# Six early weight tiles rounded by an integer addition instead of a float sum, in an attention kernel with two MLPs

## The chip, the cores and the metric

The kernel runs on one core of a Trainium2 chip. The metric is the device time of one execution in microseconds (us). Five engines work side by side, each through its own instructions in a fixed order: TensorE (PE; its weight loads are shown apart as PEld), VectorE (DVE), ScalarE (ACT), GpSimd (POOL) and SyncE (SP), which here starts most of the DMA transfers. An engine that waits for another holds back everything behind the waiting instruction in its own order.

## The reference

Attention goes through 32 memory slots per head: the key and value sums are weighted by a softmax over positions (`a`), the queries are scored against those slots, and the result `x` (4608 rows of 512) goes through a gated MLP and an ELU MLP. All inputs are float64 or float32; the three weight arrays arrive as float64.

```python
a = exp(phi - max(phi));  a = a / (sum(a) + 1e-9)
k_m = einsum('bhsm,bhsd->bhmd', a, k);  v_m = einsum('bhsm,bhsd->bhmd', a, v)
attn = softmax(q @ k_m.T / sqrt(64))
x = (attn @ v_m)                       # (8*576, 512)
x = (silu(x @ w_gate) * (x @ w_val)) @ w_out
h = x @ w_in;  return where(h > 0, h, exp(min(h, 0)) - 1) @ w_out2
```

## The kernel before

The eight batches go through a front part (`phi`, `a_T`, `kv_mm`, `kv_out`, `kv_T`: the softmax over positions and the small products that give `kT` and `vt`), a back part (`score`, `norm`, `attn`: the attention weights `at`), and the first MLP. The gate and value weights are first multiplied by `vt` (`vw`), so that the MLP's products take `at` directly (`gate1`, `val1`, through `up1`); `down1` multiplies the result by the output weights. Every large product is three products of split numbers (high by high, high by low, low by high). `vw(0, p)` of the first two pairs splits its result in PSUM: ACT copies the high part, PE subtracts it with a product by minus one (`minus`), ACT copies the rest.

A float64 weight is two 32-bit words. `words` (L122) makes a float32 pair from them: ACT reads the high word with a stride and scales it (L126); DVE shifts the exponent into place (L127), puts the sign back (L128), keeps the exponent alone (L130) and multiplies the low word by it (L131). The caller adds the two (`load_w`, L144), or, for the output weights of the first pass, splits them (`load_wo`, L171 to L173). The tiles of concern are the six that are decoded before PE is full: `wg` of pair 0 in four halves of 512 columns, `wg` of pair 1 in two tiles of 1024, and the two output tiles `wo` (in DVE's rows `wv`).

The program is written in Python order and a scheduler sets each engine's order. `tc.issue_after(x)` keeps what is written in its block behind `x`; `later()` is such a fence behind the last `h` and the first `ex`. In the first batch (`b == 0`) the list `todo` deals out the output tiles and the front part of batch 1 between the MLP's units (`tick`). Behind the second unit stands `spin` (L297): 13 products of `minus` by itself that nothing reads, then `vw(0, 1)`.

Of the kernel before, what the change touches and what calls it, by code (L numbers as in the profile page):

```python
# [8 lines left out]
F32 = mybir.dt.float32  # L9
F32R = mybir.dt.float32r  # L10
I32 = mybir.dt.int32
U32 = mybir.dt.uint32
# [26 lines left out]
def attention_moe_moe(ctx: ExitStack, tc: tile.TileContext, qT, phiT, kv, kv4, w1g, w1o, w2, out):  # L39
# [81 lines left out]
    def words(v, r):  # L121
# [9 lines left out]
        stt(out=cf, in0=lo32.bitcast(U32), scalar=2.0 ** -52, in1=cf, op0=ALU.mult, op1=ALU.mult)  # L131
        return cf

    def later():
        st = ExitStack()
        for after in last.get("h"), first.get("ex"):
            if after:
                st.enter_context(tc.issue_after(after.ins))
        return st

    def load_w(v, r):
        with later():
            cf = words(v, r)
            last["sum"] = tt(out=v, in0=v, in1=cf, op=ALU.add)  # L144

# [3 lines left out]
    def load_wg(p, k2, pool, parts=1):  # L149
        t = pool.tile([128, 2, 512], F32, tag="w", name="wg")  # L150
        WG[p][2 * k2], WG[p][2 * k2 + 1] = t[:, 0], t[:, 1]
        r = raw.pop((p, k2), None)
        if r is None:
            r = fetch_w(w1g[p, k2])
        t = t.rearrange("p i c -> p (i c)")
        n = 1024 // parts
        for i in range(parts):
            cs = slice(n * i, n * i + n)
            load_w(t[:, cs], r[:, cs])
        ahead((p, k2))  # L160

    def load_wo(u2, pool):
        hi = pool.tile([128, 2, 512], F32R, tag="w", name="woh")
        lo = (bk_p if u2 else pool).tile([128, 2, 512], F32R, tag="w", name="wol")
        for i in range(2):
            WO[2 * u2 + i] = hi[:, i], lo[:, i]
        hi, lo = (x.rearrange("p i c -> p (i c)") for x in (hi, lo))
        v = work("wv")
        with later():
            cf = words(v, fetch_w(w1o[u2]))  # L170
            act(out=hi, in_=v, func=AF.Copy)  # L171
            tt(out=v, in0=v, in1=hi.bitcast(F32), op=ALU.subtract)
            tt(out=lo, in0=v, in1=cf, op=ALU.add)  # L173

    SET = {}
    stores = []
# [53 lines left out]
    def vw(b, p, pool=None, ps=None):  # L230
        t = VW[b, p] = vx_p.tile([128, 2, 2, 512], F32R, tag="vx", name="vw")
        both = ps or pool.tile([128, 2, 512], F32, tag="at", name="pvw")
        ps = [both[:, g] for g in range(2)]

        def head(j, g):
            r, c = slice(64 * g, 64 * g + 64), slice(32 * j, 32 * j + 32)
            return mm(ps[g][c], lhsT=Bs[b].vt[r, j, :], rhs=WG[p][j][r], start=True, stop=True)

        together([lambda j=j, g=g: head(j, g) for j in reversed(range(KD)) for g in (1, 0)])
        if b >= NEG or p >= UA // 2:  # L240
            with tc.high_priority() if pool is None else nullcontext():
                act(out=t[:, 0], in_=both, func=AF.Copy)
                tt(out=t[:, 1], in0=both, in1=t[:, 0].bitcast(F32), op=ALU.subtract)
            return
        for g in range(2):
            act(out=t[:, 0, g, :], in_=ps[g], func=AF.Copy)
            mm(ps[g], lhsT=minus, rhs=t[:, 0, g, :], start=False, stop=True, skip_group_check=True)
            act(out=t[:, 1, g, :], in_=ps[g], func=AF.Copy)

    def up1(ps, w, c0, at, s0):  # L250
        cs, ss = slice(c0, c0 + 128), slice(s0, s0 + HS)
# [19 lines left out]
    def gate1(b, u, at, s0, silu):  # L271
        pg = ps_gv.tile([128, HS], F32, tag="g", name="pg")
        up1(pg, VW[b, u // 2], 256 * (u % 2), at, s0)
        s = t_p.tile([128, HS], F32, tag="s", name="s")
        if silu:
            last["gate"] = act(out=s, in_=pg, func=AF.Silu)
        else:

            act(out=s, in_=pg, func=AF.Tanh, scale=0.5)
            stt(out=s, in0=s, scalar=1.0, in1=pg, op0=ALU.add, op1=ALU.mult)  # L280
        return s

# [19 lines left out]
    class Batch:  # L302
# [18 lines left out]
        def phi(self):  # L321
            ph = self.ph
            nmx = fr_p.tile([128, 2], F32, tag="nmx", name="nmx")
            nc.vector.tensor_reduce(out=nmx, in_=ph, op=ALU.max, axis=AX.X, negate=True)
            sm = fr_p.tile([128, 2], F32, tag="sm", name="sm")
            for g in range(2):
                act(out=ph[:, g, :], in_=ph[:, g, :], func=AF.Exp, bias=nmx[:, g:g + 1],
                    accum_out=sm[:, g:g + 1])
            self.rs = fr_p.tile([128, 2], F32, tag="rs", name="rs", bufs=2)
            nc.vector.tensor_scalar_add(out=self.rs, in0=sm, scalar1=1e-9)  # L330
            nc.vector.reciprocal(out=self.rs, in_=self.rs)
# [3 lines left out]
        def a_T(self, c0):  # L335
            if c0 == 0:
                self.a = fr_p.tile([128, 9, 128], F32, tag="a", name="a")
            ps = ps_fr.tile([128, 4, 128], F32, tag="at", name="ps_aT")
            ph = self.ph.rearrange("p g s -> p (g s)")
            if c0 == 4:  # L340
                nc.tensor.transpose(out=ps[:, 0], in_=ph[:, 512:640], identity=ident)
                act(out=self.a[:, 8], in_=ps[:, 0], func=AF.Copy)
                return
            for i in range(2):
                for g in range(2):
                    s0 = 128 * (c0 + i) + 640 * g
                    nc.tensor.transpose(out=ps[:, 2 * i + g], in_=ph[:, s0:s0 + 128], identity=ident)
            act(out=self.a[:, 2 * c0:2 * c0 + 4], in_=ps, func=AF.Copy)


        def kv_mm(self, cs, start, stop):
# [22 lines left out]
        def kv_T(self):  # L374
            ps = ps_fr.tile([128, 2, 4, M], F32, tag="at", name="ps_kvT")
            for i in range(2):
                nc.tensor.transpose(out=ps[:, i].rearrange("p j m -> p (j m)"),
                                    in_=self.kvm[:, i].rearrange("p g d -> p (g d)"), identity=ident)
            self.kT = bk_p.tile([128, 4, M], F32, tag="kT", name="kT", bufs=2)
            act(out=self.kT, in_=ps[:, 0], func=AF.Copy)  # L380
            if self.b == 0:
                self.kTd = bk_p.tile([128, 4, 2, M], F32, tag="kTd", name="kTd")
                nc.gpsimd.memset(self.kTd, 0.0)
                for g in range(2):
                    r = slice(64 * g, 64 * g + 64)
                    act(out=self.kTd[r, :, g], in_=ps[r, 0], func=AF.Copy)
            self.vt = vt_p.tile([128, 4, M], F32, tag="vt", name="vt")
            act(out=self.vt, in_=ps[:, 1], func=AF.Copy)

# [43 lines left out]
        def attn(self, hf):  # L435
            if hf == 0:
                self.at = av_p.tile([128, 2, 2, S], F32R, tag="at", name="at")
            if self.b == 0 and hf == 1:
                t = ps_at.tile([128, 2, T], F32, tag="at", name="ps_ex")
                sc = self.sc.rearrange("p g s -> p (g s)")  # L440
                for i in range(2):
                    for g in range(2):
                        c0 = 256 * i + 128 * g
                        nc.tensor.transpose(out=t[:, g, 128 * i:128 * i + 128], in_=sc[:, c0:c0 + 128], identity=ident)
                for g in range(2):
                    c0 = 512 + M * g
                    last["ex"] = nc.vector.transpose(out=t[:, g, 256:HS], in_=sc[:, c0:c0 + M])
                t = t[:, :, :HS]
            else:
                t = bk_p.tile([128, 2, HS], F32, tag="ex", name="ex")  # L450
                last["ex"] = nc.vector.transpose(out=t.rearrange("p g s -> p (g s)"), in_=self.sc.rearrange("p g s -> p (g s)"))
            hi, lo = (self.at[:, i, :, HS * hf:HS * hf + HS] for i in range(2))
            act(out=hi, in_=t, func=AF.Copy)  # L453
            tt(out=lo, in0=t, in1=hi.bitcast(F32), op=ALU.subtract)  # L454

        def store_at(self):
# [99 lines left out]
    for b in range(B):  # L556
# [1 line left out]
        bk = list(back_tasks(b + 1)) if b + 1 < B else []  # L558
        fr = list(front_tasks(b + 2)) if b + 2 < B else []
        if b == 0:  # L560
            wo = [lambda u=u: load_wo(u, wo_p) for u in range(UA // 2)]
            pair = last["sum"]

            def phi1():
                with tc.issue_after(pair.ins):
                    Bs[1].phi()
                load_q(Bs[1])

            f1 = [phi1] + list(front_tasks(1)) + [lambda: Bs[2].phi()]
            for i in range(max(len(wo), len(f1))):  # L570
                todo += wo[i:i + 1] + f1[i:i + 1]
        if 2 <= b <= 5:
            bk += [lambda: load_wg(2 + (b - 2) // 2, b % 2, wa_p)]
        if b == B - 2:
# [29 lines left out]
        for hf in range(2):  # L604
            for u in range(UA):
# [2 lines left out]
                hs[hf, u] = val1(b, u, Bs[b].at, HS * hf, s, silu)  # L608
                tick()
                if (b, hf, u) == (0, 0, 1):  # L610
                    with tc.issue_after(last["pe"].ins):
                        spin(ps_kv, "at", 13)
                    vw(0, 1, G2)
                if prev:
                    down1(*prev.pop(0))
# [495 lines left out]
```

## Time and profile before

| what | value |
|---|---|
| median of 3 runs | 1432.77 us (1432.74 to 1434.7) |
| profiled execution | 1434.9 us, of which the span of the instructions is 1433.1 us |
| PE busy | 1407.0 us, 98% of the span |
| DVE busy | 1141.3 us, 80% |
| ACT busy | 857.7 us, 60% |
| mean granted clock of PE | 0.993 |
| chain that ended last | PE 89%, DMA 5%, DVE 4%, issue 1%, ACT 1% |

The profile comes from one execution. Times inside it are counted from the start of the span. PE's granted clock has two levels here, 1.0 (2.4 GHz) and 0.5 (1.2 GHz). A row of the timeline is the start, the duration, the engine, the line and operation, what is written from what with its shapes, and, where the engine stood idle before, for how long and who released it.

### The profile page before, as it was taken

Reading aid. Unit: us, or ns where it says so; the run is one execution under the profiler, and the core shown is the slowest. Engines: PE = TensorE matmul, PEld = TensorE weight load, DVE = VectorE, ACT = ScalarE, POOL = GpSimd, SP = SyncE. Lnnn points to the kernel's source line nnn. Section 1 sums busy time; section 2 is a strip of 40 time slices with the busy share of each in tenths; the row PEclk is TensorE's granted clock in tenths of the full one; section 3 lists DMA queues with packets and bytes.
Section 4 is the critical chain, followed back from the end, with each engine's and each line's share of the span. In section 5 each row is a group of like instructions: output and inputs, shape, how many; then the busy total and the mean of one; then the engine's idle time right before and its main releaser. Section 6 shows DMA issues by size and latency. Waiting matters only on the chain.

```text
span 1433.1 us, 23220 instructions
## 1 busy us (share of the span) xinstructions
PE 1407.0 (98%) x9269; PEld 1215.3 (85%) x9269; DVE 1141.3 (80%) x1460; ACT 857.7 (60%) x1251; POOL 44.8 (3%) x73
## 2 busy tenths in 40 slices
PE   5999999999999999999999999999999999999998
PEld 4688889988999999999998888888888888888887
DVE  7998887778798886886978578894898488957884
ACT  4665545544466465465657388556866588549843
POOL 0000000000000000000000000000000000000000
PEclk7999999999999999999999999999999999999999
DMA  9887522663789988888889866766676667666653
GB/s 379 316 316 282 193 75 101 220 231 136 259 248 294 298 235 253 255 246 275 280 270 367 279 203 209 268 212 198 204 272 210 202 205 250 228 205 205 208 204 132
DMA packets 89484, 337.65 MB, mean 236 GB/s; under 512 B 9376, under 2 KB 23712, under 8 KB 70048
## 3 DMA queue, kind: packets, MB, share of 16 engines
q1 hardware_dynamic: 55312, 254.04, 51.4%
q10 hardware_dynamic: 26880, 51.39, 9.8%
q0 software_dynamic: 7184, 30.74, 8.9%
q8 instruction: 73, 1.20, 0.3%
q14 instruction: 35, 0.29, 0.1%
HBM read 251.13 MB, written 85.00 MB: 235 GB/s over the span
## 4 chain that ended last, share of the span: by engine, by line
PE 89%; DMA 5%; DVE 4%; issue 1%; ACT 1%; SPq 0%; ACTq 0%; DVEq 0%
PE pu L834 12%; PE pu L833 12%; PE pu L832 12%; PE pd L834 5%; PE pd L833 5%; PE pd L832 5%; PE acc L262 4%; PE acc L260 4%; PE acc L261 4%; PE pv L255 3%; PE pg L255 3%; PE pv L257 3%; PE pv L256 3%; PE pg L257 3%; PE pg L256 3%; DMA wr<-w1g 3%
## 5 line engine op out<-in xcount | busy, mean ns | idle before, releaser
L834 PE MATMUL pu<-xhi,w 128*128 128x512 f32 x672 | 261.5, 389 | 0.0
L833 PE MATMUL pu<-xlo,w 128*128 128x512 f32 x672 | 261.4, 389 | 0.0
L832 PE MATMUL pu<-xhi,w 128*128 128x512 f32 x672 | 261.4, 389 | 0.0
L861 ACT ACTIVATE xhi<-g 128x1024 fp32r<-128x1024 f32 x120 | 126.6, 1058 | 108.4 <-PE pu L834 65.9
L862 DVE TENSOR_TENSOR xlo<-g,xhi 128x1024 fp32r<-128x1024 f32 x120 | 145.2, 1222 | 42.2 <-ACT xhi L861 42.1
L833 PEld LDWEIGHTS pu<-xlo,w 128*128 128x128 f32 x672 | 126.1, 188 | 26.3
L832 PEld LDWEIGHTS pu<-xhi,w 128*128 128x128 f32 x672 | 126.1, 188 | 26.2
L834 PEld LDWEIGHTS pu<-xhi,w 128*128 128x128 f32 x672 | 126.1, 188 | 26.1
L261 PE MATMUL acc<-hh,ws 128*128 128x288 f32 x448 | 131.8, 296 | 0.0
L260 PE MATMUL acc<-hh,ws 128*128 128x288 f32 x448 | 131.5, 295 | 0.0
L262 PE MATMUL acc<-hl,ws 128*128 128x288 f32 x448 | 128.8, 297 | 0.0
L255 PE MATMUL pv<-at,vw 128*128 128x288 f32 x384 | 116.9, 304 | 3.0 <-DVE s L280 1.2
L255 PE MATMUL pg<-at,vw 128*128 128x288 f32 x384 | 116.5, 303 | 1.9 <-ACT at L453 0.7
L722 ACT ACTIVATE hh<-gh 128x576 fp32r<-128x576 f32 x112 | 76.1, 684 | 67.6 <-PE acc L261 50.3
L257 PE MATMUL pv<-at,vw 128*128 128x288 f32 x384 | 114.2, 297 | 0.0
L256 PE MATMUL pg<-at,vw 128*128 128x288 f32 x384 | 114.0, 297 | 0.2 <-DVE at L454 0.2
L256 PE MATMUL pv<-at,vw 128*128 128x288 f32 x384 | 114.1, 297 | 0.0
L257 PE MATMUL pg<-at,vw 128*128 128x288 f32 x384 | 113.8, 297 | 0.1
L832 PE MATMUL pd<-xhi,w 128*128 128x512 f32 x288 | 112.0, 389 | 0.0
L833 PE MATMUL pd<-xlo,w 128*128 128x512 f32 x288 | 112.0, 389 | 0.0
L834 PE MATMUL pd<-xhi,w 128*128 128x512 f32 x288 | 112.0, 389 | 0.0
L852 DVE SCALAR_TENSOR_TENSOR et<-et 128x1024 f32<-128x1024 f32 x72 | 87.9, 1221 | 28.8 <-ACT et L851 28.8
(154 smaller groups left out, 3240.4 us busy)
## 6 DMA issues: line engine op xcount, KB each, us to landing
w<-dnd SPq DMA_DIRECT2D x64, 1024.0 KB, 5.0
w<-upd SPq DMA_DIRECT2D x40, 1024.0 KB, 5.7
w<-upd SPq DMA_DIRECT2D x32, 768.0 KB, 4.7
ws<-d1d SPq DMA_DIRECT2D x42, 512.0 KB, 5.0
kvr<-kv SPq DMA_DIRECT2D x32, 512.0 KB, 8.2
wr<-w SPq DMA_DIRECT2D x16, 1024.0 KB, 6.3
upd<-uw ACTq DMA_DIRECT2D x32, 512.0 KB, 6.3
dnd<-uw ACTq DMA_DIRECT2D x32, 512.0 KB, 9.1
```

What stands on the lines that cost most here:

```text
L255: mm(ps, lhsT=wh, rhs=ah, start=g == 0, stop=False)
L256: mm(ps, lhsT=wh, rhs=al, start=False, stop=False)
L257: last["pe"] = mm(ps, lhsT=wl, rhs=ah, start=False, stop=g == 1)
L260: mm(ps, lhsT=w[0][:, ms], rhs=hs[0], start=start, stop=False, skip_group_check=skip)
L261: mm(ps, lhsT=w[1][:, ms], rhs=hs[0], start=False, stop=False, skip_group_check=skip)
L262: mm(ps, lhsT=w[0][:, ms], rhs=hs[1], start=False, stop=stop, skip_group_check=skip)
L832: mm(ps, lhsT=w[0], rhs=x[0], start=start, stop=False, skip_group_check=skip)
L833: mm(ps, lhsT=w[0], rhs=x[1], start=False, stop=False, skip_group_check=skip)
L834: last["mm"] = mm(ps, lhsT=w[1], rhs=x[0], start=False, stop=stop, skip_group_check=skip)
L852: stt(out=a, in0=e, scalar=1.0, in1=a, op0=ALU.add, op1=ALU.mult)
L861: last["hi"] = act(out=hi, in_=x, func=AF.Copy)
L862: last["lo"] = tt(out=lo, in0=x, in1=hi.bitcast(F32), op=ALU.subtract)
```

## The change

Six tiles are decoded by a new function, `words_int`. ACT makes two passes, one over the high words (into the tile `wg` or `wv`) and one over the low words (a rounded integer, into `wn`); DVE shifts the first, adds the second to it as 32-bit integers, and puts the sign back. `words` stays for all later tiles. The output tiles are then split by one copy and one subtraction. The table `BEHIND` names, for each of the `wg` tiles or halves, the ACT instruction behind which either pass has to stand; for the two output tiles it is the exponential of batch 1's `phi` and the `s` of a gate. The products of `spin` are no longer issued. The output tiles are fetched by list entries of their own.

```diff
+    def words_int(v, r, one, two):
+        lo32, hi32 = r[:, :, 0], r[:, :, 1]
+        vi = v.bitcast(I32)
+        n = work("wn").bitcast(I32)[:, :r.shape[1]]
+        with tc.issue_after(last[one].ins) if one else nullcontext():
+            act(out=v, in_=hi32.bitcast(F32), func=AF.Copy, scale=2.0 ** -112)
+        with tc.issue_after(last[two].ins) if two else nullcontext():
+            act(out=n, in_=lo32.bitcast(U32), func=AF.Copy, scale=2.0 ** -29)
+        nc.vector.tensor_scalar(out=vi, in0=vi, scalar1=3, scalar2=None, op0=ALU.logical_shift_left)
+        tt(out=vi, in0=vi, in1=n, op=ALU.add)
+        return stt(out=vi, in0=hi32, scalar=-2 ** 31, in1=vi, op0=ALU.bitwise_and, op1=ALU.bitwise_or)
...
+    BEHIND = {(0, 0): [(None, None), (None, "exp")], (0, 1): [(None, "a2"), (None, None)],
+              (1, 0): [("vt", "vt")], (1, 1): [("vw", "vw")]}
...
-    def load_w(v, r):
+    def load_w(v, r, behind=None):
         with later():
+            if behind:
+                last["sum"] = words_int(v, r, *behind)
+                return
             cf = words(v, r)
             last["sum"] = tt(out=v, in0=v, in1=cf, op=ALU.add)
...
-            load_w(t[:, cs], r[:, cs])
+            load_w(t[:, cs], r[:, cs], BEHIND[p, k2][i] if p < UA // 2 else None)
...
         v = work("wv")
         with later():
-            cf = words(v, fetch_w(w1o[u2]))
+            words_int(v, raw.pop(("wo", u2)), *[("exp", "s")[u2]] * 2)
             act(out=hi, in_=v, func=AF.Copy)
-            tt(out=v, in0=v, in1=hi.bitcast(F32), op=ALU.subtract)
-            tt(out=lo, in0=v, in1=cf, op=ALU.add)
+            tt(out=lo, in0=v, in1=hi.bitcast(F32), op=ALU.subtract)
...
-            wo = [lambda u=u: load_wo(u, wo_p) for u in range(UA // 2)]
+            def fetch_wo(u2):
+                raw["wo", u2] = fetch_w(w1o[u2])
+
+            wo = [lambda: (load_wo(0, wo_p), fetch_wo(1)), lambda: load_wo(1, wo_p)]
...
-            for i in range(max(len(wo), len(f1))):
-                todo += wo[i:i + 1] + f1[i:i + 1]
+            todo += [lambda: fetch_wo(0), f1[0], lambda: None, wo[0], f1[1], f1[2], wo[1]] + f1[3:]
...
                 if (b, hf, u) == (0, 0, 1):
-                    with tc.issue_after(last["pe"].ins):
-                        spin(ps_kv, "at", 13)
                     vw(0, 1, G2)
```

The other edits only record instructions by name for the table (`last["vt"]`, `last["vw"]`, `last["exp"]`, `last["s"]` and two more). DVE's addition stands in the program as one instruction of the form `ISA wg<-wg,wn 128x2048` for 1024 words.

ACT, from the first `at` on (`wr_174` is the second `wg` tile of pair 1, `wn` its low words). Before:

```order
L126 ACTIVATE wg<-wr_174 128x1024
L453 ACTIVATE at<-ex 128x2x288
L248 ACTIVATE vw<-pvw 128x512
L246 ACTIVATE vw<-pvw 128x512
L248 ACTIVATE vw<-pvw 128x512
L279 ACTIVATE s<-pg 128x288
L424 ACTIVATE sc<-sc 128x576
```

With the change:

```order
L470 ACTIVATE at<-ex 128x2x288
L265 ACTIVATE vw<-pvw 128x512
L263 ACTIVATE vw<-pvw 128x512
L265 ACTIVATE vw<-pvw 128x512
L139 ACTIVATE wg<-wr_174 128x1024
L141 ACTIVATE wn<-wr_174 128x1024
L441 ACTIVATE sc<-sc 128x576
L296 ACTIVATE s<-pg 128x288 x2
```

The tile's pass stood ahead of `at`; it stands, as two passes, behind the last copy of `vw`, and the two `s` stand behind it.

ACT at the exponential of batch 1's `phi` (`wv` and `wn` are the first output tile). Before:

```order
L126 ACTIVATE wv<-wr 128x1024
L266 ACTIVATE hh<-h 128x288
L327 ACTIVATE ph,sm<-ph,nmx 128x576 x2
L266 ACTIVATE hh<-h 128x288
L246 ACTIVATE vw<-pvw 128x512
```

With the change:

```order
L344 ACTIVATE ph,sm<-ph,nmx 128x576 x2
L139 ACTIVATE wv<-wr 128x1024
L141 ACTIVATE wn<-wr 128x1024
L283 ACTIVATE hh<-h 128x288 x2
L263 ACTIVATE vw<-pvw 128x512
```

The output tile's passes moved from ahead of the exponentials to between them and the copies `hh` and `vw`.

PE, at the transpositions of batch 2's `phi` (`ps_aT`) and the score products (`ps_sc`). Before:

```order
L411 MATMUL ps_sc<-qr,kT 32x288 x8
L347 MATMUL ps_aT<-ident,ph 128x128 x4
L255 MATMUL pg<-at,vw 128x288
```

With the change:

```order
L274 MATMUL pv<-at,vw 128x288
L428 MATMUL ps_sc<-qr,kT 32x288 x8
L358 MATMUL ps_aT<-ident,ph 128x128
L278 MATMUL pd<-hh,wol 128x288
L279 MATMUL pd<-hl,woh 128x288
```

The transpositions no longer stand ahead of the units' next products: when the first score product stands, one more pair of units is done, and eight transpositions and the second score product are still to come.

## Rows read from the trace of the kernel before

**Rows 1.** Stretches: busy us (instructions) by engine, granted clock, DMA share, GB/s.

```profile
core 0: us, PE busy (x) PEld busy (x) DVE busy (x) ACT busy (x) POOL busy (x), PEclk, DMA share, GB/s
...
20.80:37.60 16.80, 14.75 (x69) 11.22 (x54) 15.65 (x23) 6.50 (x11) 0.00 (x0) 0.50 1.03 413
37.90:58.10 20.20, 16.75 (x191) 12.75 (x189) 18.47 (x33) 15.02 (x33) 0.00 (x0) 1.00 0.72 272
58.30:61.60 3.30, 3.30 (x26) 2.11 (x25) 3.30 (x9) 1.81 (x4) 0.00 (x0) 0.50 1.03 419
...
62.00:82.00 20.00, 19.80 (x245) 15.71 (x243) 20.00 (x40) 13.50 (x30) 0.00 (x0) 1.00 0.91 333
82.00:140.00 58.00, 57.41 (x703) 47.58 (x703) 53.34 (x108) 33.56 (x79) 0.00 (x0) 1.00 0.81 289
```

**Rows 2.** DVE's groups by line and form, 0 to 66 us: busy, mean ns.

```profile
L144 DVE TENSOR_TENSOR wg<-wg,wc 128x1024 f32<-128x1024 f32 x2 | 2.4, 1224 | 0.0
...
L268 DVE TENSOR_TENSOR hl<-h,hh 128x288 fp32r<-128x288 f32 x5 | 2.2, 455 | 0.0
...
L127 DVE TENSOR_SCALAR wc<-wg 128x1024 int32<-128x1024 int32 x2 | 1.3, 672 | 0.2 <-ACT wg L126 0.2
```

**Rows 3.** ACT's groups by line and form, 0 to 66 us.

```profile
L327 ACT ACTIVATE ph<-ph,nmx 128x576 f32<-128x576 f32 x6 | 4.6, 764 | 2.3 <-issue 1.3 <-ACT vt L388 1.0
...
L126 ACT ACTIVATE wg<-wr 128x1024 f32<-128x1024 f32 x3 | 3.5, 1154 | 2.4 <-DMA wr<-w1g 2.4
L126 ACT ACTIVATE wg<-wr 128x512 f32<-128x512 f32 x4 | 2.7, 672 | 6.1 <-DMA wr<-w1g 6.0
...
L266 ACT ACTIVATE hh<-h 128x288 fp32r<-128x288 f32 x6 | 2.5, 434 | 0.0
...
L171 ACT ACTIVATE woh<-wv 128x1024 fp32r<-128x1024 f32 x2 | 2.2, 1076 | 0.0
```

**Rows 4.** Timeline, 25 to 30 us.

```profile
25.85 1.16 ACT L126 ACTIVATE wg<-wr 128x1024 f32<-128x1024 f32 x1 [2.00 <-DMA wr<-w1g]
...
26.20 0.65 DVE L127 TENSOR_SCALAR wc<-wg 128x1024 int32<-128x1024 int32 x1
26.91 0.67 ACT L453 ACTIVATE at<-ex 128x576 fp32r<-128x576 f32 x1
...
28.79 0.75 DVE L454 TENSOR_TENSOR at<-ex,at 128x576 fp32r<-128x576 f32 x1
...
29.59 0.61 PE L256 MATMUL pg<-at,vw 128*128 128x288 f32 x1 [0.19 <-DVE at L454]
```

**Rows 5.** Timeline, 34 to 41 us.

```profile
34.76 0.61 PE L255 MATMUL pv<-at,vw 128*128 128x288 f32 x1 [1.20 <-DVE s L280]
...
36.37 3.80 PE L300 MATMUL spin<-minus 128*128 128x512 f32 x13
...
38.28 1.23 DVE L144 TENSOR_TENSOR wg<-wg,wc 128x1024 f32<-128x1024 f32 x1
...
39.41 1.35 DVE L324 TENSOR_REDUCE nmx<-ph 128x2 f32<-128x1152 f32 x1
40.22 0.18 PEld L237 LDWEIGHTS pvw<-wg,vt 64*32 64x32 f32 x16 [0.48 <-PE spin L300]
```

**Rows 6.** Timeline, 49 to 62 us.

```profile
49.46 0.81 DVE L280 SCALAR_TENSOR_TENSOR s<-s,pg 128x288 f32<-128x288 f32 x2
...
50.29 0.40 PE L255 MATMUL pv<-at,vw 128*128 128x288 f32 x1
...
55.80 0.33 PE L347 MATMUL ps_aT<-ident,ph 128*128 128x128 f32 x1 [1.20 <-ACT ph L327]
...
60.59 1.21 PE L411 MATMUL ps_sc<-qr,kT 64*32 64x288 f32 x16
```

**Rows 7.** Chain that ended last: start, us, what (half clock, then full).

```profile
59.46 0.24 PE pv L256
...
63.17 2.33 PE ps_kvm L364 x80
...
65.83 0.14 PE pg L256
```

More of the change, by code (lines that the diff above doesn't have):

```diff
@@ L241, in vw @@
             with tc.high_priority() if pool is None else nullcontext():
-                act(out=t[:, 0], in_=both, func=AF.Copy)
+                last["vw"] = act(out=t[:, 0], in_=both, func=AF.Copy)
                 tt(out=t[:, 1], in0=both, in1=t[:, 0].bitcast(F32), op=ALU.subtract)
@@ L247, in vw @@
             mm(ps[g], lhsT=minus, rhs=t[:, 0, g, :], start=False, stop=True, skip_group_check=True)
-            act(out=t[:, 1, g, :], in_=ps[g], func=AF.Copy)
+            last["vw"] = act(out=t[:, 1, g, :], in_=ps[g], func=AF.Copy)
     def up1(ps, w, c0, at, s0):
@@ L277, in gate1 @@
         else:
-            act(out=s, in_=pg, func=AF.Tanh, scale=0.5)
+            last["s"] = act(out=s, in_=pg, func=AF.Tanh, scale=0.5)
             stt(out=s, in0=s, scalar=1.0, in1=pg, op0=ALU.add, op1=ALU.mult)
@@ L326, in phi @@
             for g in range(2):
-                act(out=ph[:, g, :], in_=ph[:, g, :], func=AF.Exp, bias=nmx[:, g:g + 1],
-                    accum_out=sm[:, g:g + 1])
+                last["exp"] = act(out=ph[:, g, :], in_=ph[:, g, :], func=AF.Exp, bias=nmx[:, g:g + 1],
+                                  accum_out=sm[:, g:g + 1])
             self.rs = fr_p.tile([128, 2], F32, tag="rs", name="rs", bufs=2)
@@ L347, in a_T @@
                     nc.tensor.transpose(out=ps[:, 2 * i + g], in_=ph[:, s0:s0 + 128], identity=ident)
-            act(out=self.a[:, 2 * c0:2 * c0 + 4], in_=ps, func=AF.Copy)
+            last["a2"] = act(out=self.a[:, 2 * c0:2 * c0 + 4], in_=ps, func=AF.Copy)
         def kv_mm(self, cs, start, stop):
@@ L387, in kv_T @@
             self.vt = vt_p.tile([128, 4, M], F32, tag="vt", name="vt")
-            act(out=self.vt, in_=ps[:, 1], func=AF.Copy)
+            last["vt"] = act(out=self.vt, in_=ps[:, 1], func=AF.Copy)
         def score(self, hf):
@@ L452, in attn @@
             hi, lo = (self.at[:, i, :, HS * hf:HS * hf + HS] for i in range(2))
-            act(out=hi, in_=t, func=AF.Copy)
+            last["at"] = act(out=hi, in_=t, func=AF.Copy)
             tt(out=lo, in0=t, in1=hi.bitcast(F32), op=ALU.subtract)
```

## The prediction

> **What bounds the kernel now.** I read the busy times first (the table above), then the start in short stretches, then its timeline. PE is busy 98% of the span: nearly all of the time is PE's own work, which the change leaves as it is but for the 13 idle products. So only the start can give time. There the stretches show three kinds of loss [rows 1]. From 20.8 to 37.6 us PE has the lower granted clock, 0.50 (1.2 GHz), and DVE is the busier engine, 15.65 of 16.8 us. From 37.9 to 58.1 PE has the full clock but works only 16.75 of 20.2 us. From 58.3 to 61.6 PE is always busy, at 0.50 again. From 62 on PE is full: 19.80 of 20 us, then 57.41 of 58, so at most 0.8 us of waiting is left between 62 and 140. The question is thus at what time PE stands where it stood at 62 us.
>
> **What a decode costs.** Before, a tile of 1024 columns costs DVE a shift and a mask of one form (0.67 each) and three passes of 1.22 [rows 2]: 5.0 us. The change leaves a shift, the integer addition and one pass with the sign. No row shows the addition. It takes two tiles in and one out, as L144 does, 1.22; but it is listed with 2048 elements, so its other end is twice that, 2.45. Below 1.22 no two-input pass of that length lies in the trace. I take 1.22, since two 1024-word reads and one write are what L144 also has; that makes 3.1 us, 1.9 less. A half saves about half of that, 1.0; an output tile loses a mask and a pass too, 1.9. In all DVE loses 4 x 1.0 + 4 x 1.9 = 11.6 us of work. ACT gains a pass for each: 4 x 0.67 + 4 x 1.15 = 7.3 us [rows 3]. ACT's pass over the low words has no row; it reads as many words at the same stride, so I take 1.15. The row below it is `woh` with 1.08, and above it I set two `woh`, 2.15, though nothing in the rows asks for it; at that end each pass on the path adds 1.0.
>
> As to the addition's price, the Trainium skill (VectorE: DVE Perf Modes, "What auto-detection actually checks") says that 16-bit streams with unit step go two elements per cycle in a two-source operation. By that rule 2048 halves take as long as 1024 words; without it the sum below would be that of the third rival. No run yet shows which.
>
> **Up to 28 us.** The four halves are waited for less than before, but what starts PE's first weight product also needs `vt`, and ACT makes both passes of the next tile, 2.3 us, while DVE prepares the softmax. So I take nothing here, and the first row that moves is `at`: ACT's copy was held until 26.91 by the pass that began at 25.85, and DVE's until 28.79 by three decode passes [rows 4]. Now DVE has a shift and an addition ahead, 26.20 + 0.65 + 1.22 = 28.05. **Gain 0.74.**
>
> **28 to 38 us.** PE then runs six products ahead of the subtraction by which ACT gets the last `vw` copy; at 0.24 us a product [rows 7] the copy ends at about 31.4. Behind it, in ACT's order, stand the two passes of the second `wg` tile (to 33.6), an exponential and the two `s` (34.9). DVE, waiting for the low words, adds from 33.6 to 34.8, sums the softmax, makes both `s` (36.2) and the sign (1.22): the tile is ready at 37.4. PE's value products, which wait for the first `s`, start at 35.9 instead of 34.76: **a loss of 1.1** [rows 5]. But `vw(0, 1)`, which waits for the tile and no longer for the 13 idle products, starts at 37.45 instead of 40.22: **a gain of 2.8**. Of these the tile gives 2.1 (39.51 less 37.4); the idle products, 3.80 us of PE's time, hide only the remaining 0.7.
>
> **38 to 50 us: the gain goes.** DVE's maximum of batch 1's `phi` starts at 37.3 instead of 39.41. From there ACT and DVE make one chain. Maximum 1.35 and two exponentials: 40.25. Then the two passes of the output tile, 2.3: 42.55. Two `hh` and, behind each, `hl` on DVE: 43.8 [rows 2, 3]. Before, one pass lay ahead of the exponentials, in a wait, and the two `hh` did not stand behind it. On DVE follow two short transpositions, shift, addition, the low part of `at` (0.75) and the sign: 47.9; ACT's `woh` 49.0, DVE's `wol` 50.2, and then the `s` of unit 2, at 50.2 instead of 49.46 [rows 6]. **A loss of 0.7 in place of the gain.** ACT's chain also covers what PE does meanwhile, even at half clock: from 43.9 it has some 5.5 us of products at that clock to do by 49.6.
>
> **50 to 62 us.** Before, PE resumed at 50.29 with 80 small products already done in the wait, but lost time later: it waited for batch 2's `phi` (its transposition at 55.80 waited 1.20 for ACT) and then ran at half clock until its second score product ended at 61.80 [rows 1, 6]. In the new order PE takes 12 products from 50.65 at 0.14 (1.6 us), the 80 small ones (2.33), 18 more (2.4) and two transpositions: 57.25 [rows 7]. There it waits for the second output tile: ACT's high pass behind the second `s` ends at 53.1, DVE's shift, addition and sign with three small passes between at 57.1, `woh` at 58.2, and the `h` that frees PE's next bank, behind the maximum of batch 2, at 58.8. Six products and a score product end at 60.35. Against the order before, one score product and eight transpositions (1.55) are missing and one product (0.14) is ahead: 60.35 + 1.4 = 61.76 against 61.80. **Nothing gained.**
>
> **After 62 us** DVE has no decode left, where before two passes of the second output tile were still to come. Of PE's waits up to 140, 0.8 us in all, I take all as gone; the other end is nothing.
>
> SP fetches the same tiles; the first `wg` tile of later use now goes ahead of batch 2's `phi`, which the path above already has late enough.
>
> **The sum** is 0.0 to 62 us and -0.8 after: 1434.9 - 0.8 = 1434.1 for an execution like the profiled one. That one lies 2.1 above the median; taken off, **1432.0 us**. About 0.2%, 2.9 us, is what a measurement here can tell from no change. With no wait gained later and up to a microsecond of error in each chain the forecast's own range is 1430.0 to 1434.6.
>
> **Rivals.**
>
> *The gain at 37.45 is kept.* If ACT's passes, or the DVE work between them, fit into ACT's waits better than my sum has them, the 2.8 us arrive at 62, and PE does not fall to half clock before it, which costs 3.3 / 2 = 1.65. That gives 1432.8 - 4.4 = 1428.4. For it: ACT is busy only 6.50 of 16.8 and 15.02 of 20.2 us [rows 1], and DVE loses 11.6 us. Against: the passes are pinned to fixed places with `s` and `hh` behind. Chance 0.36.
>
> *PE stays at half clock* (slower). Before, the clock was 0.50 all through the stretch to 37.6, though PE worked 14.75 of its 16.8 us, and rose within the idle products, after PE had worked without a break from 34.76 on [rows 1, 5]. Now PE has a pause of 3 us before 35.9 and more pauses to 43.9. Until 50 the ACT chain hides that. From there it decides: if the clock is still 0.50 when PE resumes at 50.65, the 6.6 us of products to 57.25 become 13.2, less the 1.6 us that PE waits there anyway: +5.0, 1437.0. The same if it falls again and stays. Against: from 43.9 to 49.6 PE is busy almost without a break, as it was from 34.76 until the clock rose. Chance 0.13. The Trainium skill (TensorE: Matmul & The Clock Gate, Part 1) calls the lower clock the default and says that activity releases it. That speaks against leaving out idle products; the trace agrees in so far as the clock rose during them.
>
> *The addition takes 2.45.* Then the tile of pair 1 and both output tiles are 1.22 later, all on the path: +3.7, 1435.7. For it: the 2048 elements. Chance 0.08.
>
> That the passes do not stand where the table puts them is excluded by the listing above.
>
> **How the numbers follow.** Forecast 0.43, kept gain 0.36, half clock 0.13, slow addition 0.08. Faster by over 0.2% (below 1429.9): most of the second case and the forecast's lower edge, 0.36. Slower (above 1435.6): the last two, and a little of the forecast's upper edge, 0.22. Within 0.2%: 0.42. From 1427.8 to 1436.0 leaves out the better part of the half-clock case and the lowest tenth of the kept gain, less than 2 in 10.
>
> **What would show it.** DVE's addition of 1024 words in its groups, 1.22 or 2.45; `vw(0, 1)` starting near 37.5; the `s` of unit 2 near 50; the granted clock from 38 to 62; the wait for the second output tile at 57 to 59. The forecast is wrong if `hh` does not wait for ACT's two output passes, or if PE stands at the state of 62 us over 3 us earlier or later.

## The result and the profile after

The changed kernel takes 1440.60 us (median of 4 runs, 1439.33 to 1442.3), the kernel before beside it 1433.01 (median of 4 runs): a ratio of 1.0051, with a 95% interval of 1.0034 to 1.0069. It is **slower by 0.5%**, 7.6 us. Forecast was no change, and the time lies 4.6 us above the range's upper end. The profiled execution took 1441.19 us, its span is 1439.4, 6.3 more than before. Of its engines PE was busy 1404.8 us and DVE 1132.9, 8.4 less than before.

The stretches of the changed kernel (columns as in rows 1):

```profile
core 0: us, PE busy (x) PEld busy (x) DVE busy (x) ACT busy (x) POOL busy (x), PEclk, DMA share, GB/s
20.00:62.00 42.00, 32.24 (x268) 24.66 (x261) 34.19 (x58) 27.72 (x51) 0.00 (x0) 0.76 0.88 340
62.00:82.00 20.00, 17.20 (x213) 13.98 (x212) 16.45 (x33) 11.83 (x26) 0.00 (x0) 0.91 0.93 329
82.00:100.00 18.00, 17.45 (x230) 13.54 (x228) 16.46 (x32) 11.43 (x27) 0.00 (x0) 1.00 0.78 275
...
82.00:140.00 58.00, 55.84 (x692) 45.89 (x691) 51.88 (x102) 33.59 (x78) 0.00 (x0) 1.00 0.78 270
```

Of the kernel before, the two stretches that rows 1 do not have:

```profile
20.00:62.00 42.00, 36.04 (x291) 27.02 (x289) 39.12 (x65) 23.93 (x47) 0.00 (x0) 0.76 0.88 347
...
82.00:100.00 18.00, 17.41 (x228) 13.71 (x229) 18.00 (x38) 10.93 (x25) 0.00 (x0) 1.00 0.95 353
```

From 20 to 62 us PE is idle 42 - 32.24 = 9.76 us. Before it was idle 42 - 36.04 = 5.96, and 3.80 of its work were the idle products [rows 5]: 9.76 too, at the same mean clock of 0.76. So between 20 and 62 us nothing was gained and nothing lost. (Up to 20 us PE works 7.64 us, in the kernel before 8.17.) Then PE lacks 2.80 us of 20 and 2.16 of 58, where before it lacked 0.20 and 0.59 [rows 1], and between 76 and 81 us it falls to half clock once more:

```profile
62.00:76.00 14.00, 11.75 (x163) 10.49 (x161) 12.07 (x25) 8.70 (x20) 0.00 (x0) 1.00 0.90 308
76.00:81.00 5.00, 4.45 (x42) 2.49 (x43) 3.42 (x7) 3.00 (x7) 0.00 (x0) 0.66 0.99 376
```

That costs some 4.45 x (1 - 0.66) = 1.5 us, an estimate from the second row. Together the idle time and the clock make 4.2 + 1.5 = 5.7 of the 6.3 us. DVE tells the same from the other side: before it had no free moment from 62 to 100 us (20.00 of 20 and 18.00 of 18), now it has 5.1 us free. Neither engine is the bound there any more; they wait for each other.

The operations of the change, DVE's and ACT's groups of the changed kernel up to 66 us:

```profile
L143 DVE CUSTOM_DVE_ANT_0 wg<-wg,wn 128x1024 uint16<-128x1024 uint16 x4 | 2.8, 692 | 1.5 <-ACT wn L141 1.3
...
L143 DVE CUSTOM_DVE_ANT_0 wg<-wg,wn 128x2048 uint16<-128x2048 uint16 x2 | 2.5, 1225 | 0.4 <-ACT wn L141 0.3
...
L144 DVE SCALAR_TENSOR_TENSOR wg<-wr,wg 128x1024 int32<-128x1024 int32 x2 | 2.4, 1216 | 0.0
```

```profile
L141 ACT ACTIVATE wn<-wr 128x1024 int32<-128x1024 uint32 x4 | 4.5, 1118 | 0.0
```

They cost what the forecast had. A row of the waits that follow is who waited for whom, the sum in us, how often, and the longest. PE's waits from 62 to 140 us, after:

```profile
PE ps_kvT L394 <- ACT kvm L388: 2.8, 1, 2.8
PE pg L272 <- DVE s L297: 1.6, 2, 0.9
PE ps_kvm L381 <- ACT s L296: 0.5, 1, 0.5
```

and before:

```profile
PE ps_kvm L364 <- issue: 0.8, 1, 0.8
```

The longest of them in the timeline of the changed kernel, from the last transposition of batch 2's `phi` to PE's next weight product:

```profile
68.75 0.27 PE L358 MATMUL ps_aT<-ident,ph 128*128 128x128 f32 x1
...
69.05 0.38 SPq L326 DMA_DIRECT2D ph<-phiT  x1
...
71.34 2.40 PE L381 MATMUL ps_kvm<-kvr,a 64*32 64x128 f32 x80
...
72.98 1.35 DVE L341 TENSOR_REDUCE nmx<-ph 128x2 f32<-128x1152 f32 x1 [0.58 <-DMA ph<-phiT]
...
74.36 0.78 ACT L344 ACTIVATE ph<-ph,nmx 128x576 f32<-128x576 f32 x1 [1.49 <-DVE nmx L341]
...
75.89 0.60 ACT L388 ACTIVATE kvm<-ps_kvm,rs 128x128 f32<-128x128 f32 x2
...
76.55 0.44 PE L394 MATMUL ps_kvT<-ident,kvm 128*128 128x128 f32 x2 [2.80 <-ACT kvm L388]
76.92 1.58 PE L254 MATMUL pvw<-wg,vt 64*32 64x512 f32 x16
```

Batch 3's `phi` can be fetched only when the last transposition of batch 2 has left its buffer, at 69.05 (before: 62.33). Its maximum waits for the transfer, its exponential for the maximum, and the copy `kvm` of batch 2, whose products were done at 73.7, stands behind that exponential in ACT's order. PE stands idle 2.80 us, and its next weight product runs for the most part at half clock (1.58 us; at 83.19 the same product takes 1.09). Why batch 2 is late can be read upstream, in the same kernel:

```profile
50.59 1.11 ACT L141 ACTIVATE wn<-wr 128x1024 int32<-128x1024 uint32 x1
51.61 0.26 ACT L359 ACTIVATE a<-ps_aT 128x128 f32<-128x128 f32 x1
...
53.02 2.40 PE L381 MATMUL ps_kvm<-kvr,a 64*32 64x128 f32 x80
...
55.40 1.17 ACT L126 ACTIVATE wg<-wr 128x1024 f32<-128x1024 f32 x1 [1.24 <-DMA wr<-w1g]
...
56.47 0.59 ACT L388 ACTIVATE kvm<-ps_kvm,rs 128x128 f32<-128x128 f32 x2
...
58.72 0.78 ACT L344 ACTIVATE ph<-ph,nmx 128x576 f32<-128x576 f32 x1
...
60.73 0.33 PE L364 MATMUL ps_aT<-ident,ph 128*128 128x128 f32 x1
```

Batch 1's last copy `a` stands behind a pass of the second output tile, its 80 small products start at 53.02 (before: 47.95), its `kvm` stands behind a `wg` pass that waits 1.24 us for a transfer, and batch 2's exponential and transpositions follow (60.73 against 55.80 [rows 6]). The copies `kvm` of batch 1 and 2 thus come at 56.47 and 75.89; in the kernel before they came at

```profile
50.47 0.63 ACT L371 ACTIVATE kvm<-ps_kvm,rs 128x128 f32<-128x128 f32 x2 [2.26 <-PE ps_kvm L364]
65.61 0.63 ACT L371 ACTIVATE kvm<-ps_kvm,rs 128x128 f32<-128x128 f32 x2 [0.76 <-PE ps_kvm L364]
```

One profile among the experiments, that of e5, was taken with the clock granted at 0.56 over its whole span; its stages are not read, and the kernel was run again as e13.

### The profile page after: what moved, and what is told of

Read it like the earlier page. It is cut to its first block, busy times and chain, and to the rows that moved or that the text cites. A ratio compares the mean times of both kernels' runs of the same rounds, so it can differ in the third digit from the quotient of the medians.

```text
span 1439.4 us, 23192 instructions
## 1 busy us (share of the span) xinstructions
PE 1404.8 (98%) x9256; PEld 1213.3 (84%) x9256; DVE 1132.9 (79%) x1444; ACT 864.0 (60%) x1259; POOL 44.8 (3%) x73
## 4 chain that ended last, share of the span: by engine, by line
PE 86%; DVE 6%; DMA 4%; ACT 2%; issue 1%; ACTq 0%; SPq 0%; DVEq 0%
PE pu L851 12%; PE pu L850 12%; PE pu L849 12%; PE pd L851 5%; PE pd L850 5%; PE pd L849 5%; PE acc L279 4%; PE acc L277 4%; PE acc L278 4%; PE pg L272 3%; PE pv L272 3%; PE pg L273 3%; PE pg L274 3%; PE pv L273 3%; PE pv L274 3%; DMA wr<-w1g 3%
```

## The experiments

Theories: the one wait for `kvm` (e1); the missing idle products and the clock (e2, e3); the places that the table sets (e4, e6 to e8, e11); the position of batch 1's and 2's front parts in the order, measured by when `kvm` is copied (e5, e9 to e13). Behind each measured time, a median, stands its ratio to the kernel before, run beside it, and in brackets the 95% interval of that ratio.

### e1: batch 3's exponential behind batch 2's `kvm`

```diff
-                last["exp"] = act(out=ph[:, g, :], in_=ph[:, g, :], func=AF.Exp, bias=nmx[:, g:g + 1],
-                                  accum_out=sm[:, g:g + 1])
+                with tc.issue_after(last["kvm"].ins) if self.b == 3 else nullcontext():
+                    last["exp"] = act(out=ph[:, g, :], in_=ph[:, g, :], func=AF.Exp, bias=nmx[:, g:g + 1],
+                                      accum_out=sm[:, g:g + 1])
```

(`last["kvm"]` is set in `kv_out`.) Of the whole order four rows of ACT and one of DVE change.

> The changed kernel, with one fence more: the exponentials of batch 3's phi stand behind the scaled copies kvm of batch 2 on ACT. Only these four rows of ACT and one row of DVE change places. Theory (the exponentials, late by their transfer, hold kvm and so PE for 2.8 us, and the pause lowers PE's clock): PE's wait before kvT near 76 us falls from 2.8 to below 1 us, the clock stays at 1.0 from 75 to 85 us, and the time falls by 3 to 5 us, to 1436 to 1438. Rival (the loss is spread over the new order, and this wait only shows it): less than 1.5 us.

Measured: 1439.18 us, 1.0040 [1.0024, 1.0056]. The wait and the fall of the clock are gone, the time almost stays. PE's waits from 62 to 140 us, and the stretch:

```profile
PE pg L272 <- DVE s L297: 2.5, 3, 1.5
PE pg L272 <- ACT vw L259: 1.4, 1, 1.4
PE ps_kvm L382 <- ACT s L296: 0.8, 1, 0.8
PE ps_sc L429 <- ACT kT L398: 0.8, 1, 0.8
PE ps_kvT L395 <- ACT kvm L389: 0.7, 1, 0.7
```

```profile
62.00:82.00 20.00, 17.11 (x224) 13.66 (x230) 16.79 (x33) 12.24 (x27) 0.00 (x0) 1.00 0.92 325
```

PE works no more of 62 to 82 than in the changed kernel, and of 82 to 140 less (54.65 us against 55.84); other waits took the place of the one. The wait that the profile names is a place where the loss shows, not its cause. What came back, 0.11% or 1.6 us, is about what the clock had cost there; the intervals of the two ratios overlap, so it is not clear of noise. The theory's 3 to 5 us are out.

### e2 and e3: the idle products

e2 issues the 13 products again in the changed kernel; e3 leaves them out of the kernel before, and changes nothing else in the program.

```diff
                 if (b, hf, u) == (0, 0, 1):
+                    with tc.issue_after(last["pe"].ins):
+                        spin(ps_kv, "at", 13)
                     vw(0, 1, G2)
```

> The changed kernel with the 13 idle products put back. The scheduler then sets another order, in which kvm of batch 2 stands ahead of the exponentials of batch 3. Rival (PE at half clock from 21 to 50 us is what costs): the clock is at 1.0 from about 41 us and the time falls by over 3 us for that, seen before 62 us. Theory: before 62 us PE gains at most 1 us, since ACT's chain sets the pace there; what is gained lies after 62 us, from the order: 1435 to 1438.

> The kernel before without the 13 idle products, nothing else. Here too the scheduler sets another order up to some 150 us. Rival (half clock): slower by 3 us or more, with the clock at 0.50 to beyond 45 us. Theory: DVE's decode holds vw(0, 1) until 39.5 us anyway, so the products hide 0.7 us; within 2 us of the kernel before, unless the new order brings a wait of its own after 62 us.

Measured: e2 1439.34 us, 1.0039 [1.0024, 1.0054]; e3 1438.88 us, 1.0035 [1.0023, 1.0047]. In e2 the products raise the clock, to 1.00 from 44 to 48 us where it is 0.50 in the changed kernel, but the time stays, and both forecasts for e2 are out. In e3, where nothing else was edited, the time rises by 5 us, and the rival's two signs appear: over 3 us, and a clock of 0.50 until 46 us. But the idle products' own place shows little of the loss: PE waits there for the tile instead,

```profile
PE pvw L237 <- DVE wg L144: 5.0, 2, 3.8
```

and from 20 to 62 us the mean clock is 0.76, as before, and PE is idle 11.09 us, 1.3 more than before with the idle products counted as idle. Behind 62 us more is lost: from 62 to 300 PE lacks 5.1 us, before 2.0. What e3 changes besides is the order: the scheduler reckons the products' length, and without it deals out what follows, up to about 150 us, in another order. So e3 does not separate the products from the order; e5 comes closer to that.

### e4, e7, e8: which places cost

e4 drops all places; e7 those of the output tiles; e8 those of the gate weights.

```diff
-            load_w(t[:, cs], r[:, cs], BEHIND[p, k2][i] if p < UA // 2 else None)
+            load_w(t[:, cs], r[:, cs], (None, None) if p < UA // 2 else None)
...
-            words_int(v, raw.pop(("wo", u2)), *[("exp", "s")[u2]] * 2)
+            words_int(v, raw.pop(("wo", u2)), None, None)
```

(e4 has both, e7 the second alone, e8 the first alone.)

> The changed kernel without the table of places: no pass has to stand behind a named instruction. The scheduler sets kvm of batch 2 ahead of the exponentials of batch 3, and the passes of the first output tile ahead of batch 1's exponentials. Theory: 1434 to 1437, faster than the change by the wait at 76 us. Rival (the places are right and the integer decode itself costs): as slow as the change, 1440.

> The changed kernel without the places of the two output tiles' passes (those of the gate weights stay). e4, without any place, was 5.8 us under the changed kernel. If the output tiles' places (behind batch 2's exponential and behind the activation) cost that: 1434 to 1436 us. If those of the gate weights do: 1439 to 1441 us.

> The changed kernel without the places of the gate weights' passes (those of the output tiles stay). If the output tiles' places cost the 5.8 us: 1439 to 1441 us. If those of the gate weights do: 1434 to 1436 us. If each costs a part, e7 and e8 both lie between 1436 and 1439 us.

Measured: e4 1434.83 us, 1.0012 [1.0002, 1.0022]; e7 1437.41, 1.0023 [1.0014, 1.0032]; e8 1444.60, 1.0072 [1.0060, 1.0085]. All six tiles by integers, without idle products and without a place, thus cost 0.12%, by the interval at most 0.22%. The output tiles' places cost most: 0.60% without the others (e4 to e8), 0.28% beside them (e7 to the changed kernel). The gate weights' places cost 0.11% by themselves (e4 to e7) and save 0.21% beside the others (e8 to the changed kernel). Such terms do not add: each place changes the order after it. The 0.60% is clear of noise by a wide margin and the 0.28% barely; the intervals of the kernels behind the 0.11% and the 0.21% overlap. e4 came as its theory had it; e7 lies between its two ranges, and e8 above all that were set for it.

e4 shows a second thing, in its start:

```profile
20.00:62.00 42.00, 33.34 (x319) 25.95 (x307) 38.00 (x67) 31.36 (x58) 0.00 (x0) 0.88 0.95 376
62.00:82.00 20.00, 17.38 (x241) 13.02 (x239) 18.48 (x36) 13.03 (x28) 0.00 (x0) 1.00 0.92 343
```

PE's 33.34 us at a mean clock of 0.88 make 29.3 us of work at full clock, an estimate; the changed kernel's 32.24 at 0.76 make 24.5, and the kernel before stood level with it. So e4 is some 5 us ahead at 62 us, and that is most of its 5.8 us over the changed kernel: from 62 to 82 PE lacks as much in both (2.62 and 2.80). Over the kernel before e4 has nothing of it at the end: from 62 to 140 PE lacks 3.8 us, where before it lacked 0.8.

### e5, e6 and e13: the decode in the old order

e5 decodes the gate weights by integers with their places (the four halves of pair 0 and the two tiles of pair 1; the expectations name the halves alone), the output tiles and the list as before, without the idle products. With these the scheduler comes back to the order before: from PE's row 119, DVE's row 58 and ACT's row 33 on, at about 40 us, the listings are the same. e6 is e5 without the places, and its order differs.

```diff
-            words_int(v, raw.pop(("wo", u2)), *[("exp", "s")[u2]] * 2)
+            cf = words(v, fetch_w(w1o[u2]))
             act(out=hi, in_=v, func=AF.Copy)
-            tt(out=lo, in0=v, in1=hi.bitcast(F32), op=ALU.subtract)
+            tt(out=v, in0=v, in1=hi.bitcast(F32), op=ALU.subtract)
+            tt(out=lo, in0=v, in1=cf, op=ALU.add)
...
-            todo += [lambda: fetch_wo(0), f1[0], lambda: None, wo[0], f1[1], f1[2], wo[1]] + f1[3:]
+            for i in range(max(len(wo), len(f1))):
+                todo += wo[i:i + 1] + f1[i:i + 1]
```

> The four halves of the gate weights by the integer addition with their places, the two output tiles and the list of tasks as in the kernel before, no idle products. TensorE then meets batch 2's front products and its key and value product at the same place among the unit products as in the kernel before. Theory A (what costs time is that batch 2's front chain stands behind more unit products and then finds TensorE with nothing to do): 1431 to 1434 us, within 0.2% of before or a little under, TensorE 19.5 to 20 us busy of 62:82. Theory B (what costs time is that the idle products are gone, through the clock): 1437 to 1440 us, with the granted clock at or below 0.9 of 41:62 and TensorE short of work there. Theory C (the places of the gate weights themselves hold ScalarE up): 1436 to 1440 us, with waits of TensorE for ScalarE between 30 and 82 us.

> As e5, without the places of the gate weights' passes: only the four halves of the gate weights are decoded by integers, nothing else is changed but the idle products left out. The order then puts batch 2's key and value product behind about 5 us more unit products than the kernel before. Theory A: 1435 to 1438 us, above e5 by 2 us or more, with TensorE short of work between 62 and 82. Theory C (the places cost by themselves): under e5 by 3 us or more. Theory B: equal to e5 within 1 us, both at 1437 to 1440.

> e5 once more, for a profile: the one of e5 was taken with the clock granted at 0.56 over the whole span. From TensorE's row 119 on the order of the kernel before stands here unchanged, on VectorE from row 58 and on ScalarE from row 33; the idle products are gone and the four halves of the gate weights are added as integers. Theory A (the order after about 40 us sets the end): 1433 to 1436 us, batch 1's kvm copy at 50 to 51 us, batch 2's at 65 to 66, VectorE 19.5 us or more busy of 62:82 and TensorE 19.5 or more at a clock of 1.00, as in the kernel before. Rival (the order does not matter, e5 was near the kernel before by chance of its clock): kvm copies late as in the changed kernel (56 and 75 us) or TensorE under 18 us busy of 62:82.

Measured: e5 1434.98 us, 1.0008 [0.9999, 1.0017]; e13, the same kernel, 1435.09, 1.0008 [0.9999, 1.0018]; e6 1435.61, 1.0012 [1.0003, 1.0021]. The stretches of e13:

```profile
20.00:62.00 42.00, 30.67 (x290) 22.52 (x282) 35.26 (x60) 26.09 (x51) 0.00 (x0) 0.80 0.89 353
62.00:82.00 20.00, 19.45 (x238) 14.79 (x236) 20.00 (x40) 13.17 (x29) 0.00 (x0) 1.00 0.88 324
82.00:100.00 18.00, 17.14 (x226) 13.43 (x227) 18.00 (x36) 10.65 (x25) 0.00 (x0) 1.00 0.94 352
```

and the copies of batch 1 and 2 there:

```profile
50.23 0.63 ACT L389 ACTIVATE kvm<-ps_kvm,rs 128x128 f32<-128x128 f32 x2 [2.20 <-PE ps_kvm L382]
65.03 0.61 ACT L389 ACTIVATE kvm<-ps_kvm,rs 128x128 f32<-128x128 f32 x2
```

DVE is full from 62 to 100 as before, PE nearly so, and the copies come where they came before (50.47 and 65.61). The idle products and the float decode of the gate weights are gone, and it shows neither as a gain nor as the loss. That is theory A, though e5's time lies 1 us above its range and e13's 19.45 just under its 19.5; theories B and C are out. Of e6 no theory is right as a whole: it is within A's range, but lies 0.6 above e5, not 2.

### e9, e10: only the order changed, in the kernel before

The copy `kvm` of batch 1 gets a place: in e9 behind the first pass of the second output tile, in e10 behind that tile's `woh`. The decode, the list and the idle products are those of the kernel before.

```diff
-                act(out=self.kvm[:, :, g, :], in_=self.kvp[g], func=AF.Copy, scale=self.rs[:, g:g + 1])
+                with tc.issue_after(last["wo"].ins) if self.b == 1 else nullcontext():
+                    act(out=self.kvm[:, :, g, :], in_=self.kvp[g], func=AF.Copy, scale=self.rs[:, g:g + 1])
```

(`last["wo"]` is set at the pass in `words` in e9, at `woh` in e10.)

> The kernel before with one place added: ScalarE's copy of batch 1's key and value product (kvm) comes behind the first pass of the second output tile, not ahead of it. Decoding, list and idle products are as before. In the runs so far that copy began at 50.47 us in the kernel before, at 50.5 to 50.9 in the three kernels within 1% of its time below 1436, and at 53.6 to 56.5 in the five at 1437 and more. Theory A (the place of that copy in time sets the end; the decoding does not): the copy at 52.5 to 53 us and 1434.5 to 1437 us, 1 to 3 above before. Theory B (the loss comes from the decoding's own instructions or from the missing idle products): no more than 1 us above before.

> As e9, but the copy comes behind the rounding of the second output tile on ScalarE, at 57 to 59 us, 7 to 8 us later than in the kernel before. Theory A: 1439 to 1443 us, as late at the end as the changed kernel or later, though nothing of the decoding was changed. Theory B: within 1 us of before.

Measured: e9 1439.38 us, 1.0035 [1.0022, 1.0048]; e10 1438.59, 1.0040 [1.0028, 1.0052]. One place, with no arithmetic changed, costs 0.35 and 0.40%, most of a loss like the changed kernel's 0.51%. So an order alone can cost that much; theory B is out. But the size is not that of the delay: e9 lies above theory A's range and e10 just under its own. In e9:

```profile
52.24 0.61 ACT L372 ACTIVATE kvm<-ps_kvm,rs 128x128 f32<-128x128 f32 x2
66.69 0.62 ACT L372 ACTIVATE kvm<-ps_kvm,rs 128x128 f32<-128x128 f32 x2 [1.03 <-PE ps_kvm L364]
88.27 0.61 ACT L372 ACTIVATE kvm<-ps_kvm,rs 128x128 f32<-128x128 f32 x2
116.99 0.60 ACT L372 ACTIVATE kvm<-ps_kvm,rs 128x128 f32<-128x128 f32 x2
```

The copy is 1.8 us later than before, batch 4's (the fourth row) 10.3 later (before: 106.74). In e10 the copy comes at 58.09, 7.6 later, and the time is the same within a microsecond. The order that follows decides, not the delay. (e9's expectation counts three kernels below 1436 us with an early copy; one of them is e7, whose runs gave 1437.41, with the copy at 50.85. So the measure had failed once already.)

### e11, e12: the front part put first

e11 is the changed kernel with the first output tile's passes behind batch 1's first copy `a` and the second's behind batch 1's `kvm`. e12 drops the table and instead puts the second output tile's passes and batch 2's exponential behind that `kvm`.

```diff
-            words_int(v, raw.pop(("wo", u2)), *[("exp", "s")[u2]] * 2)
+            words_int(v, raw.pop(("wo", u2)), *[("a2", "kvm")[u2]] * 2)
...
-            todo += [lambda: fetch_wo(0), f1[0], lambda: None, wo[0], f1[1], f1[2], wo[1]] + f1[3:]
+            todo += [lambda: fetch_wo(0), f1[0], lambda: None, f1[1], wo[0], f1[2], f1[3], f1[4], wo[1]] + f1[5:]
```

(That is e11; e12 has `(None, "kvm")`, the list with `wo[0]` ahead of `f1[1]`, and e1's fence for batch 2.)

> The changed kernel with other places for the two output tiles: the first tile's passes behind batch 1's transposed phi (the first copy a) instead of behind its exponential, the second tile's behind batch 1's kvm instead of behind the activation; all six tiles by integers, places of the gate weights kept, no idle products. Theory A: the copy kvm of batch 1 comes 1 to 5 us earlier than the 56.47 us of the changed kernel, and the time falls with it by as much: 1434 to 1439 us. Rival (what costs in the changed kernel are the places of the gate weights, or the six tiles' passes as such): 1440 to 1442 us.

> All six tiles by integers without the table's places, and instead two places that put batch 1's chain first: the second output tile's passes and batch 2's exponential both come behind batch 1's kvm. Theory A: that copy at 46 to 49 us, 2 to 4 us earlier than in the kernel before, and 1429 to 1433 us, under both kernels. Rival (beyond the state of the kernel before, batch 1's chain is not what is late; the next ones, the scores and vw of batch 1 or batch 2's chain, are): 1433.5 to 1436 us in spite of the earlier copy.

Measured: e11 1439.66 us, 1.0042 [1.0030, 1.0054]; e12 1436.03, 1.0017 [1.0008, 1.0026]. In e11 the copies come at 53.89 and 69.05, 2.6 and 6.8 us ahead of the changed kernel, and at most some 0.1% of the time comes of it, which is not clear of noise; the time lies between the two ranges. The loss has moved: PE is full from 62 to 82 and lacks 1.6 us of 82 to 140, but from 20 to 62 it is idle 13.55 us (changed kernel: 9.76), and from 140 to 300 it lacks 2.9 (0.25). In e12 the copies come earlier than in the kernel before:

```profile
46.31 0.61 ACT L389 ACTIVATE kvm<-ps_kvm,rs 128x128 f32<-128x128 f32 x2
62.10 0.61 ACT L389 ACTIVATE kvm<-ps_kvm,rs 128x128 f32<-128x128 f32 x2
87.62 0.61 ACT L389 ACTIVATE kvm<-ps_kvm,rs 128x128 f32<-128x128 f32 x2
```

```profile
20.00:62.00 42.00, 34.21 (x403) 26.78 (x388) 38.86 (x70) 31.62 (x60) 0.00 (x0) 0.92 0.95 377
62.00:82.00 20.00, 15.63 (x152) 12.11 (x151) 16.30 (x33) 11.51 (x26) 0.00 (x0) 1.00 0.88 337
```

By the estimate made for e4, PE is some 7 us ahead of the changed kernel at 62 us (34.21 x 0.92 = 31.5). Still it lacks 4.37 us from 62 to 82, and the lead is gone by batch 3 (85.28 before). The rival named there holds, at the edge of its range: ahead of the old state, something else is late. What that is was not found. As a measure of the time, the moment of these copies fell with e9 to e12. No version beats the kernel before; e4, e5 and e6 come nearest.

## Why the prediction was wrong

**What a decode costs: right.** The addition takes 1.225 us (1.22 forecast), ACT's pass over the low words 1.12 (1.15). The Trainium skill (VectorE: DVE Perf Modes, "Side-by-side: where the cycles go for N=2048 bf16") gives about 1224 ns for 2048 bf16 elements at two per cycle; the trace's row has 1225 for this addition, which agrees. The third rival is out. DVE's busy time fell by 8.4 us and not by 11.6. But count times mean of the decode's own rows up to 66 us makes 34.2 us before and 22.1 after, 12.1 less, so the price was right. Rows that follow closely overlap in the trace and count once (the addition from 27.18 us on takes 1.23, and `at` starts at 28.32), which explains at least part of the difference. Two slips of the working change nothing: the shortest two-input pass of that length there is 1.205 us (L173), and 26.20 + 0.65 + 1.22 is 28.07.

**Up to 62 us: right nearly by the row.** DVE's `at` at 28.32 (28.05 forecast), PE's value products at 36.41 (35.9), `vw(0, 1)` at 38.15 (37.45), each 0.3 to 0.7 us late:

```profile
28.32 0.75 DVE L471 TENSOR_TENSOR at<-ex,at 128x576 fp32r<-128x576 f32 x1
...
36.41 0.61 PE L272 MATMUL pv<-at,vw 128*128 128x288 f32 x1 [3.06 <-DVE s L297]
...
38.15 1.89 PE L254 MATMUL pvw<-wg,vt 64*32 64x512 f32 x16
```

The gain there is lost in ACT's chain, as forecast, and the `s` of unit 2 comes at 50.73 (50.2). The score product ends at 60.81 (60.35). The rival of half clock, as it was priced, is out as well: from 45 to 50 the clock was 0.50, but the `s` of unit 2, which the chain ends with, came only 0.5 us later than forecast, and from 50 to 62 it is 1.00. The rival that keeps the gain falls with the same rows. Kernels that do keep it at 62 us, e4 and e12, end no earlier than the kernel before (0.12 and 0.17% slower). So the step that the forecast shares with this rival, that a gain at 62 us is a gain at the end, does not hold either.

**The step that failed is the last of "50 to 62 us".** It set two states equal because PE had as much work behind it in both: "one score product and eight transpositions (1.55) are missing and one product (0.14) is ahead: 60.35 + 1.4 = 61.76 against 61.80". In PE's own hours that was right: from 20 to 62 us idle time and mean clock are equal, to the hundredth by chance. But the two kinds of work are not alike. The eight transpositions are the head of a line through ACT, SP, a transfer, DVE and ACT again, which gives batch 2's `kT` and `vt`, and behind it batch 3's `phi`; the unit products done instead lead to nothing that is waited for. PE had thereby spent the work that was to cover that line. **"After 62 us", -0.8, was 5.7 the other way**: 4.2 us of idle time up to 140 and 1.5 of clock. The size and the place of that loss are measured; the covering is a reading of the rows, and no run shows it by itself: without the wait (e1), and with the line 6.8 us earlier (e11), the time stayed within 0.1%. The prediction had quoted the missing transpositions, and dismissed batch 2's `phi` with the remark that the path had it late enough.

**No rival named this.** All three priced the places up to 62 us. That the order after it is dealt anew, by a scheduler that reckons with every length and every place, had no price, though the listings showed it. e9 shows what it can cost with no arithmetic changed: 0.35%, some 5 us. e13 shows the converse: with the old order from about 40 us on, the integer decode of the gate weights and the missing idle products cost 0.08%, with an interval from -0.01 to 0.18%. And e4 has all six tiles by integers at 0.12%. So the loss comes with the places, those of the output tiles above all (e4 to e8), and the order they brought, not with the decode.

**Left open** is what makes one order good. Three measures failed: the single wait (e1), the time of batch 1's copy (e10, e12), that of batch 2's (e11). What sorts the kernels is the copy `kvm` of the last batch: 193.98 us before, 194.5 to 195.0 in e13, e4, e6 and e12, 196.9 in e7, 199.0 to 204.4 in all the others. So the loss is made by then; that measures it and does not explain it. No run keeps the order of the kernel before with the output tiles by integers as well.

## What to carry to other kernels

When a scheduler sets the order, do not compare two states by how much work an engine has done alone: the same amount at 62 us was followed by a loss of 5.7 us here, and 5 to 7 us more of it by no gain. That the lines started through other engines are what counts is likely, and not shown. Before pricing a change of a few instructions, look how far its order differs from the old one, and give a re-dealt order a price of its own in both directions: here twelve orders lay between +0.1% and +0.7%, and none below (they are no sample: two were made to delay a copy). To learn what an operation costs, look for a variant that changes it and leaves the order as it was.

## What the runs showed of the hardware

An int32 addition of two 1024-word tiles on VectorE stands in the trace as a custom operation on 2048 16-bit elements, and takes 1.225 us, no more than the float addition it replaces (1.224 [rows 2]). For 512 words it takes 0.692. ACT reads the low words as integers at a stride of two, scales them and writes them as integers in 1.12 us, as fast as its float pass (1.15 [rows 3]). That PE's idle products pay by the clock is shown by no run. From 20 to 62 us the mean granted clock is 0.76 in the kernel before, 0.76 in e3 and 0.80 in e13, both without them (in e13 the gate weights are decoded by integers too); in the changed kernel it is 0.76 without and 0.84 with them (e2). The time of e13 and of e2 is within 0.12% of that of its partner, and the 0.35% of e3 came with another order.
